# Zero products and overwritten products on TensorE in the opening of a linformer-attention and mixer kernel: more of the first kind at the start, three moved by one step, fewer of the second kind

## The chip, the cores and the metric

The kernel runs on one core of a Trainium2 chip. The metric is the device time of one execution in microseconds (us); the lower, the better. Runs of the kernel before took 430.44 to 431.93 us, with a median of 431.54 us over five runs.

## The reference

Two blocks follow each other for a batch of 8 sequences of 1024 rows, with 8 heads of 64 columns (512 columns in all):

```
k_proj = E @ k            # E, F: 64 x 1024; per batch and head 64 x 64
v_proj = F @ v
attn   = softmax(q @ k_proj^T / 8)         # 1024 x 64 per head
x      = attn @ v_proj                     # heads side by side: 1024 x 512
h      = relu(x^T @ w_tok1) @ w_tok2       # mixing over the 1024 rows
u      = x + h^T
out    = u + relu(u @ w_ch1) @ w_ch2       # mixing over the 512 columns
```

Inputs and output are float32; the kernel's products are in bfloat16 with float32 sums.

## The kernel before, in words

All inputs come in by DMA queues: E on SP's, F on ScalarE's, and everything else on GpSimd's queue, which casts float32 to bfloat16 on the way. Batch 0 comes in four head pairs; for each pair k, then q, then v, 256 KB each as stored. After the last pair come w_tok1 and w_tok2, the first half of w_ch1, and then the loads of batch 1, the rest of w_ch1 and w_ch2. The q load of batch 1 reuses the buffer of batch 0's q, so it waits for the last turn of that q.

The order of the work is written out by hand in `ORDER` (lines 17 ff.); each name stands for a small step, and every engine takes its own instructions from it in this order. Batches overlap: the up and down products of batch b run between the attention and the row mixing of the batches after it. Batch 0 has no earlier batch to run beside, so its opening runs by head pair (number after the dot):

- `EF` (`eft`, L232): eight TensorE transposes of E and F, cast to bfloat16 by VectorE (L239) and ScalarE (L240), into PSUM, and one VectorE copy to `EFT` (L233).
- `KP` and `VP` (L246, L251): eight products each of `EFT` with k or v, 64 output rows wide, for one head pair. `Ka` copies the k projection out to `kprojs`, `KT` transposes it (L271), `Ba` and `Bd` put it into the block-diagonal `kbd`. `Va` and `Vd` put the v projection into `vbd`.
- `QT` (L401): eight transposes of q; `QC` copies them out (`qT`).
- `S0`, `S1` (L455): scores of a head; `E0`, `E1`: exponential on ScalarE; `O0`, `O1` (L300): product with `vbd`, and the division on VectorE (L306, L307), into `x_sb`.
- `M1` (L470), `N0`, `N1` (L483), `UT` (L497): the row mixing of one pair's columns with w_tok1 and w_tok2, and transposes of its result; `F0` to `F3` and the steps `m0.n` (L538): the products with w_ch1.

Two kinds of products on TensorE have results that nobody reads. `busy` (L227) multiplies a part of the still zero `kbd` with itself, 512 columns, into a PSUM bank of its own: eight times at the very start, as soon as `kbd` is cleared, and three times in the step `W1`. And `FILL` (L422) gives a number of 512-column products of `EFT` with the identity (L437) for a `KP` or `VP` step: they write into the very bank that the step then starts anew, so they are overwritten. They come in front of the step's own products, whose first one waits for the load.

Of the kernel before, what the change touches and what calls it, by code (L numbers as in the profile page):

```python
# [14 lines left out]


ORDER = """
EF KP.0 Ka.0 W1 KT.0 Ba.0 Bd.0 QT.0 KP.1 QC.0 VP.0 Ka.1 S1.0 QT.1 KT.1 QC.1 VP.1 lv2 Bd.1 Ba.1
Vd.0 KP.2 S0.0 Va.0 E1.0 Vd.1 O1.0 Ka.2 QT.2 Va.1 KT.2 S0.1 E0.0 S1.1 E1.1 QC.2 Ba.2 Bd.2 O0.0
VP.2 E0.1 S0.2 KP.3 Va.2 E0.2 Vd.2 O1.1 S1.2 Ka.3 O0.1 E1.2 KT.3 Bd.3 QT.3 QC.3 VP.3 O1.2 Ba.3  # L20
S0.3 Vd.3 O0.2 E0.3 M1.0 RR.0 M1.1 RR.1 Va.3 S1.3 O0.3 M1.2 N1.0 U1.0 N0.0 U0.0 E1.3 O1.3 RR.2
# [71 lines left out]
def kernel(  # L93
# [16 lines left out]
    KP = E.shape[0]  # L110
# [111 lines left out]
    def busy(psf, n):  # L222

        zero = kbd.rearrange("p h k -> p (h k)")
        w_ps = psf("w_ps")
        for _ in range(n):
            nc.tensor.matmul(w_ps, zero[:, 0:P], zero[:, 0:512], start=True, stop=True)  # L227
# [4 lines left out]
            nc.tensor.transpose(e_ps[:, si * P : (si + 1) * P], EF_sb[:, si::SC], ident)  # L232
        nc.vector.tensor_copy(out=EFT.rearrange("p s k -> p (s k)"), in_=e_ps)  # L233

    busy(c_ps, 8)

    first = work.tile([P, 1], BF16, tag="first", name="first", bufs=1)
    nc.scalar.activation(out=first, in_=kbd[:, 0, 0:1], func=ACT.Copy)
# [173 lines left out]
    def first_ps(name, dt=F32):  # L412

        return pinned_ps(name, dt) if pinned["on"] else any_ps(name, dt)
# [4 lines left out]
        st["qT", 0] = work.tile([P, H, 4, P], BF16, tag="qT", name="qT", bufs=1)  # L419


    FILL = {("KP", 1): 4, ("KP", 2): 2, ("KP", 3): 2, ("VP", 3): 3}  # L422

    def first_op(op, hp, eng="A"):

# [8 lines left out]
        elif op in ("KP", "VP"):  # L434
            st[key(op)] = ps_ = first_ps("kv_ps")
            for _ in range(FILL.get((op, hp), 0)):
                nc.tensor.matmul(  # L437
# [476 lines left out]
```

## Time and profile before

| what | value |
|---|---|
| median of five runs | 431.54 us (430.44 to 431.93) |
| the profiled execution | 431.93 us |
| its span, first to last instruction | 430.1 us |
| TensorE busy | 416.3 us (97% of the span) |
| VectorE, ScalarE, GpSimd busy | 302.3, 203.5, 205.5 us |
| mean granted TensorE clock | 0.992 |
| chain that ended last | TensorE 92%, VectorE 4%, DMA 1% |
| DMA | 60.79 MB, mean 141 GB/s |

The chain is found by going back from the last instruction, at each step to what released it. The granted clock is the share of full speed that TensorE's throttle let through. Matmuls are pipelined, so that the duration of a single one (0.38 us for 512 columns at full speed) is longer than the time from one start to the next; a row of several in the chain shows the latter. In a list of stretches, the columns after the limits are the length, the busy time of an engine with the number of its instructions, the clock, the DMA share (over 1 where transfers overlap), and GB/s.

### The profile page before, as it was taken

The numbers are of one execution on the slowest core, as the hardware profiler recorded it, in microseconds if no ns is written. First come the engines' busy times: TensorE is split into PE (matmuls) and PEld (weight loads), VectorE is DVE, ScalarE is ACT, GpSimd is POOL, SyncE is SP. The second block draws the span as 40 slices with busy tenths as digits, with TensorE's granted clock in tenths as the row PEclk, the third lists the DMA queues.
The fourth block names the chain that finished last, engine by engine and source line by source line (L and its number), as shares of the span: only waits on it lengthen the run. The fifth ranks groups of instructions, "written<-read, shape, count | busy, mean of one in ns | idle before, by whom it ended". The sixth has DMA issues, their size and how long they took to land.

```text
span 430.1 us, 7705 instructions
## 1 busy us (share of the span) xinstructions
PE 416.3 (97%) x3034; PEld 271.9 (63%) x3066; DVE 302.3 (70%) x510; ACT 203.5 (47%) x362; POOL 205.5 (48%) x148
## 2 busy tenths in 40 slices
PE   6989999999999999999999999999999999999996
PEld 2667457765478644785457844786448854785485
DVE  2466468868936778868768677777779766947862
ACT  2436684157553555334753366334652356314621
POOL 8250014144652648553565635535356626654652
PEclk8899999999999999999999999999999999999999
DMA  9999999969979999952999289464914320242014
GB/s 168 208 206 205 207 165 175 211 131 212 202 109 203 158 240 174 168 98 50 250 170 215 91 152 155 73 171 96 163 37 90 107 99 2 53 146 98 2 49 148
DMA packets 89332, 60.79 MB, mean 141 GB/s; under 512 B 55760, under 2 KB 84944, under 8 KB 89296
## 3 DMA queue, kind: packets, MB, share of 16 engines
q0 software_dynamic: 29200, 29.36, 43.7%
q1 hardware_dynamic: 60016, 30.68, 30.2%
q8 instruction: 24, 0.39, 0.4%
q10 hardware_dynamic: 80, 0.26, 0.3%
q14 instruction: 12, 0.10, 0.1%
HBM read 59.24 MB, written 16.78 MB: 177 GB/s over the span
## 4 chain that ended last, share of the span: by engine, by line
PE 92%; DVE 4%; DMA 1%; issue 1%; ACT 1%; POOL 0%; DVEq 0%; ACTq 0%
PE be L661 19%; PE be L606 17%; PE ga L661 9%; PE ga L606 9%; PE h_ps L347 5%; PE u_ps L363 5%; PE g_ps L538 5%; PE al L661 4%; PE al L606 4%; PE kv_ps L246 4%; PE ou_ps L300 4%; PE sco L287 2%; DMA EF_in<-in_F_dram 1%; DVE S L530 1%; PE qt_ps L401 1%; PE u_ps L483 1%
## 5 line engine op out<-in xcount | busy, mean ns | idle before, releaser
L570 ACT ACTIVATE K<-be 128x512 f32<-128x512 f32 x116 | 65.7, 598 | 66.1 <-PE be L661 38.6
L661 PEld LDWEIGHTS <-g 128*128 128x128 bf16 x768 | 74.5, 98 | 16.2 <-issue 1.0
L661 PEld LDWEIGHTS <-S 128*128 128x128 bf16 x576 | 55.9, 98 | 11.7 <-issue 0.4
L292 ACT ACTIVATE attnT<-sco 128x512 bf16<-128x512 f32 x56 | 33.5, 598 | 50.8 <-PE sco L287 39.2
L606 PEld LDWEIGHTS <-wc 128*128 128x128 bf16 x336 | 32.1, 98 | 36.2 <-DVE g L612 0.4
L697 POOL TENSOR_TENSOR K<-K,u_sb 128x512 f32<-128x512 f32 x16 | 19.0, 1186 | 67.6 <-ACT K L570 67.6
L661 PE MATMUL be<-wc,g 128*128 128x256 bf16 x384 | 48.5, 273 | 0.7 <-DVE g L528 0.6
L570 ACT ACTIVATE K<-ga 128x512 f32<-128x512 f32 x58 | 32.8, 600 | 33.4 <-PE ga L661 29.9
L307 DVE TENSOR_TENSOR x_sb<-ou_ps,rdn 128x512 bf16<-128x512 f32 x64 | 44.2, 691 | 2.2
L606 PE MATMUL be<-uT,wc 128*128 128x512 bf16 x168 | 44.7, 379 | 0.2
L366 DVE TENSOR_TENSOR u_sb<-u_ps,x_sb 128x512 bf16<-128x512 f32 x56 | 37.1, 683 | 9.4 <-PE u_ps L363 8.1
L606 PEld LDWEIGHTS <-uS 128*128 128x128 bf16 x252 | 23.9, 98 | 25.7
L612 DVE CUSTOM_DVE_ANT_0 g<-be,K 128x512 bf16<-128x512 f32 x42 | 27.3, 687 | 16.7 <-PE be L606 16.6
L524 POOL TENSOR_TENSOR S<-g 128x1024 bf16<-128x1024 bf16 x7 | 14.9, 2124 | 46.6 <-DVE g L612 46.6
L645 ACT ACTIVATE g<-be 128x512 bf16<-128x512 f32 x42 | 23.8, 596 | 26.1 <-PE be L606 26.1
L528 POOL TENSOR_TENSOR g<-g 128x1024 bf16<-128x1024 bf16 x13 | 28.9, 2227 | 14.2 <-DVE S L524 14.0
L612 DVE CUSTOM_DVE_ANT_0 g<-al,K 128x512 bf16<-128x512 f32 x42 | 27.6, 687 | 10.9 <-PE al L606 10.6
L707 POOL TENSOR_TENSOR K<-K,u_sb 128x512 f32<-128x512 f32 x16 | 20.5, 1283 | 30.0 <-ACT K L570 30.0
L363 PE MATMUL u_ps<-R_sb,wt 128*128 128x512 bf16 x104 | 29.9, 379 | 0.6 <-DVE u_sb L366 0.3
L306 DVE RECIPROCAL rdn<-ou_ps 128x8 f32<-128x8 f32 x64 | 13.1, 204 | 24.6 <-PE ou_ps L300 24.3
L530 POOL TENSOR_TENSOR S<-g,S 128x1024 bf16<-128x1024 bf16 x13 | 28.4, 2187 | 0.9 <-ACT K L570 0.7
L347 PE MATMUL h_ps<-x_sb,wt 128*128 128x512 bf16 x102 | 28.1, 379 | 0.3
(102 smaller groups left out, 777.4 us busy)
## 6 DMA issues: line engine op xcount, KB each, us to landing
out_dram<-o SPq DMA_DIRECT2D x30, 512.0 KB, 3.1
q_sb<-in_q_dram POOLq DMA_DIRECT2D x7, 1024.0 KB, 11.4
k_sb<-in_k_dram POOLq DMA_DIRECT2D x7, 1024.0 KB, 11.7
v_sb<-in_v_dram POOLq DMA_DIRECT2D x7, 1024.0 KB, 12.3
wc<-in_moe_w_ch_dram POOLq DMA_DIRECT2D x4, 384.0 KB, 13.7
wc<-in_moe_w_ch_dram POOLq DMA_DIRECT2D x2, 768.0 KB, 26.4
k_sb<-in_k_dram POOLq DMA_DIRECT2D x4, 256.0 KB, 7.0
q_sb<-in_q_dram POOLq DMA_DIRECT2D x4, 256.0 KB, 7.5
```

What stands on the lines that cost most here:

```text
L292: nc.scalar.activation(out=at, in_=sco, func=ACT.Exp, scale=scale)
L307: nc.vector.tensor_tensor(out=st["x", b][:, :, h * D : (h + 1) * D].rearrange("p (b k) d -> p b k d", b=2), in0=ov[:, :, :, 0:D], in1=rdn[ ...
L347: nc.tensor.matmul(st["h", b], wt1[:, s, t * P : (t + 1) * P], st["x", b][:, s, :], start=(s == 0), stop=(s == SC - 1),)
L363: nc.tensor.matmul(u_ps, wt2[:, t, s::SC], st["R", b][:, t, :], start=(t == 0), stop=(t == TC - 1))
L366: nc.vector.tensor_add(out=st["u", b][:, s, :], in0=u_ps, in1=st["x", b][:, s, :])
L528: eng.tensor_sub(out=a21, in0=a11, in1=a21)
L530: eng.tensor_sub(out=s4, in0=a12, in1=s2)
L570: nc.scalar.activation(out=t, in_=x, func=ACT.Copy)
L606: nc.tensor.matmul(acc, l[:, dc, i * P : (i + 1) * P], r[:, :, dc, :], start=start and dc == 0, stop=stop and dc == 1, skip_group_check=True,)
L612: nc.vector._custom_dve(TENSOR_ADD_SAT, out=o, in0=x, in1=y, s0=3.0e38, s1=0.0)
L645: nc.scalar.activation(out=g_part(b, i + e, 1, 1, 0)[:, 0], in_=be[e], func=ACT.Relu)
L661: nc.tensor.matmul(acc[:, e * HF : (e + 1) * HF], l[:, lc + c, l0 + (2 * j + e) * P : l0 + (2 * j + e + 1) * P], r[:, rc + c, r0 : r0 + HF ...
```

## The change

It alters three numbers and one position:

- the zero products at the very start become 13 instead of 8;
- the step `W1`, three zero products, stands between `EF` and `KP.0` instead of behind `Ka.0`. On TensorE its products then come after the transposes of E and F and ahead of the first k projection;
- the overwritten products become two instead of four ahead of `KP.1`, none instead of two ahead of `KP.2`, one instead of two ahead of `KP.3`; the three ahead of `VP.3` stay.

In all TensorE has as many instructions as before: five zero products more and five overwritten products fewer. The lists of the other engines and of the DMAs keep their order.

```diff
@@ ORDER @@
-EF KP.0 Ka.0 W1 KT.0 Ba.0 Bd.0 QT.0 KP.1 QC.0 VP.0 Ka.1 S1.0 QT.1 KT.1 QC.1 VP.1 lv2 Bd.1 Ba.1
+EF W1 KP.0 Ka.0 KT.0 Ba.0 Bd.0 QT.0 KP.1 QC.0 VP.0 Ka.1 S1.0 QT.1 KT.1 QC.1 VP.1 lv2 Bd.1 Ba.1
...
-    busy(c_ps, 8)
+    busy(c_ps, 13)
...
-    FILL = {("KP", 1): 4, ("KP", 2): 2, ("KP", 3): 2, ("VP", 3): 3}
+    FILL = {("KP", 1): 2, ("VP", 3): 3, ("KP", 3): 1}
```

## The prediction

> **What bounds the kernel now.** I read three views of the profile before: the chain of waits over the first 60 us, the clock by stretches, and the DMA issues one by one. Over the whole span the page gives TensorE 92% of the chain, and every slice after the first few is 9 of 10 busy, so what moves TensorE's work in the first 25 us forward moves the end, unless a load stops it. The chain, as start, duration and piece:
>
> ```profile
> 6.68 0.73 PE e_ps L232 x8
> 7.41 0.02 issue
> 7.43 0.70 DVE EFT L233
> 8.14 0.04 issue
> 8.18 1.06 PE kv_ps L246 x8
> 9.24 1.40 PE w_ps L227 x3
> 10.64 0.22 PE kt_ps L271 x2
> 10.86 0.97 PE qt_ps L401 x8
> 11.82 1.71 PE kv_ps L437 x4
> 13.53 0.67 PE kv_ps L246 x5
> ...
> 20.39 0.43 PE kv_ps L437 x2
> ```
>
> See two things. The three zero products (L227) and the four overwritten products (L437) are on the chain, 1.40 and 1.71 us. And four 512-column products take 1.71 us at 11.82, two take 0.43 us at 20.39: 0.43 us each, then 0.215. So the array runs at half speed until some time after 13.5. The stretches, as from:to, length, TensorE busy, granted clock, DMA share, GB/s:
>
> ```profile
> 0.95:4.36 3.41, 2.90 (x7) 1.00 0.61 157
> 4.36:7.77 3.41, 1.13 (x10) 1.00 1.21 197
> 7.77:11.19 3.42, 3.01 (x17) 0.50 1.22 201
> 11.19:14.60 3.41, 3.41 (x25) 0.50 1.24 206
> 14.60:18.01 3.41, 3.26 (x41) 1.00 1.24 205
> ...
> 21.43:24.84 3.41, 2.29 (x27) 1.00 1.09 207
> ```
>
> The clock is halved from 7.77 to 14.60, which are the limits I found by narrowing the stretches. The 1.00 of the first row is only the absence of a record: the zero products there begin 0.43 us apart, half speed. From 4.36 to 7.77 TensorE was busy for 1.13 us and the clock fell at its end; from 21.43 to 24.84 it was busy for 2.29 us and the clock stayed.
>
> The loads (issue time plus landing time) set the floor. The last v pair is the one that matters:
>
> ```profile
> 10.46 0.71 POOL L165 DMA_DIRECT2D v_sb<-in_v_dram  x1 [0.60 <-DMA k_sb<-in_k_dram]
> ...
> v_sb<-in_v_dram POOLq DMA_DIRECT2D x1, 256.0 KB, 11.4
> ```
>
> It lands at 10.46 + 11.4 = 21.9, and VP.3 begins at 24.51. In the same way: k of pair 1 lands at 10.2 (KP.1 begins 13.46), q of pair 1 at 11.5 (QT.1 15.01), v at 12.8 (VP.1 15.71), k of pair 2 at 14.0 (KP.2 16.81), q 15.3 (QT.2 17.83), v 16.5 (VP.2 19.43), k of pair 3 at 17.9 (KP.3 20.75), q 19.1 (QT.3 23.31). Every load is 2.5 to 4.2 us early: today TensorE is behind its loads.
>
> **What the Trainium skill says.** "TensorE: Matmul & The Clock Gate", Part 1: the array's clock is halved by default; a free-running window of some 3.4 us with enough activity gives the full clock, an idle one takes it back. The trace agrees: its limits 4.36, 7.77, 14.60 are 3.41 and 2 x 3.41 apart, and 4.36 - 3.41 = 0.95 is where the first filled window began. The same page, Part 4: a transpose on TensorE does not count as busy in the same way. The trace neither proves nor excludes it: the window that failed had 0.41 us of zero products beside 0.72 of transposes. I therefore count windows with and without them. The page gives no level of activity; the trace brackets it.
>
> **The change, part by part.**
>
> 1. *Five more zero products ahead of the turned E and F.* Before, eight begin at 1.46 and end at 4.77; TensorE then idles 1.91 us until F is loaded and cast (6.68). With the clock up at 4.36 some seven run at 0.43 and six at 0.216: 1.46 + 7 x 0.427 + 6 x 0.216 = 5.75. The idle time hides them: cost 0. If the window begins late and all run at half speed, 1.46 + 13 x 0.427 = 7.01, 0.33 past 6.68: cost between 0 and 0.35 us. I take 0. They can't gain by themselves; their use is in the window 4.36 to 7.77, which holds 1.0 us more.
>
> 2. *The three zero products (W1) go ahead of KP.0.* They now follow the transposes at 7.41 and need no EFT. TensorE waits there for the 0.70 us copy of EFT until 8.18, a hole of 0.77. At full speed 3 x 0.216 = 0.65 fits: cost 0. At half speed 1.28 overruns by 0.5. What goes: 1.40 us behind KP.0. There KT.0 would have waited for Ka.0 anyway (the cast of kprojs, 9.28 to 9.70) and could begin at 9.73 instead of 10.64, so 0.9 us is the gain at today's clock.
>
> 3. *The clock.* Busy time from 4.36 to 7.77 becomes 1.13 + 1.0 (zero products) + 0.35 (W1 before 7.77) = 2.5 us, over the 2.29 that kept it later; without transposes 1.7 against about 1.5 there. I take it that the clock stays. Then KP.0 (8.18) takes the 0.63 us that KP.2 shows, Ka.0 ends at 9.3, KT.0 at 9.45, QT.0 takes 0.45 instead of 0.97 and ends at 9.9.
>
> 4. *Fewer overwritten products.* KP.1: two instead of four, at full speed 0.43 instead of 1.71. KP.1 is ready at 10.35, its k landed at 10.2: 3.2 us earlier than 13.53. From here the loads lead: QT.1 can't begin before 11.5, VP.1 12.8, KP.2 14.0, and so on to VP.3 at 21.9. The two products ahead of KP.2 (0.32 and a 0.15 us gap) and one of two ahead of KP.3 (0.22) are gone; in this case they fall into waits for loads: gain 0. VP.3's three stay, ahead of its wait.
>
> *The sum.* From VP.3 on, TensorE has the old work in the old order: 24.51 - 21.95 = 2.6 us earlier (0.05 for the wake-up, as between F's landing and its cast). **What is late next:** w_tok1 lands at 23.9; the first product of M1.0 moves from 26.74 to 24.15, just behind it. w_tok2 lands at 26.5 (N1.0's turn, 29.86 to 27.3), the first half of w_ch1 at 30.3 (35.8 to 33.2), q of batch 1 at 35.4 (39.1 to 36.5), v of batch 1 at 49.4 (kv1 52.5 to 49.9), the last of w_ch2 at 55.6, used near 60. All clear by 0.2 us or more. The moves touch no instruction of ScalarE, GpSimd, VectorE's order or SP, and no DMA. The next batch's loads wait for TensorE and come earlier with it.
>
> The profiled execution took 431.93 us, of which 1.8 lies outside its span of 430.1. 431.93 - 2.6 = **429.3 us**. The median of the five runs is 431.54; that execution is the slowest of the five (430.44 to 431.93), as would fit windows that begin elsewhere in each run. Against the median it is 2.2 us, 0.5%. The floor by landings is the same for any phase of the window; with 0.4 us for the scatter of landings the case's own range is 428.7 to 429.9. A measurement of this kernel can tell about 0.2%, 0.86 us, from no change.
>
> **Rivals.**
>
> *B: the clock falls inside the stretch where loads lead.* From 11.19 to 14.60 there would be S1.0, QT.1, KT.1, VP.1 and half of KP.2: about 2.1 us busy, and only 1.1 without transposes. That lies between the 1.13 (0.41) that lost the clock and the 2.29 (1.5) that kept it; the removed products ahead of KP.2 stood just there. The work from 14.6 to VP.3 is 5.9 us at full speed in the 7.3 us up to 21.9. One window at half speed does 1.7 us of it: VP.3 at 22.25, 429.7 us. Two: VP.3 at 24.0, 431.4 us, no change.
>
> *C: the clock falls at 7.77 as before and returns at 14.60.* W1 ends at about 8.4, KP.1 begins at 11.9 instead of 13.5. By 14.60 the lead, 1.5 us at half speed, is worth 0.75, and the fills of KP.2 and KP.3 add 0.55: -1.3, 430.6 us. For it: the bracket is only a bracket. Against: 2.5 us busy.
>
> *D, slower: the clock falls at 7.77 and the thinned stretch can't raise it again.* The window 7.77 to 11.19 with 3.01 us busy, W1's three products in it, did not raise it; the next one, with 1.71 us of dense overwritten products, did. With two of those four gone and the rest 64-column products and transposes, it may stay low. Each further us at half speed costs 0.5 us: back at 18.01, -1.3 + 1.7 = +0.4; back at 21.43, +2.1: 434.0 us. It decides from a return later than about 18.2. For it: what is removed is just what raised the clock. Against: it needs the loss at 7.77 first.
>
> That the change does nothing it says is no rival: the instruction lists show the products moved.
>
> **How the numbers follow.** The full chain holds: 0.66. B 0.13, half of it at 429.7, half at 431.4. C 0.07, on the edge of 0.2%. D 0.14. Faster: 0.64 + 0.07 + 0.04 = 0.75; same: 0.02 + 0.06 + 0.03 = 0.11; slower 0.14. The range runs from 428.7 up to 431.6, over B and C, and leaves out D and the tails of the first case.
>
> **What would show it.** Right: the halved clock before about 5 us only, or never recorded; the zero products of L227 after 7.41 0.216 apart; KP.0 at 8.2 lasting 0.63; TensorE waiting for loads of k, q and v between 11 and 22; VP.3 at 21.9 to 22.0, M1.0 at 24.2. Wrong: a clock of 0.50 beyond 7.77 (C, D) or again after 14 (B); VP.3 after 22.5; or a later wait for w_tok1, batch 1's v or w_ch2 that takes the lead back.

## The result and the profile after

| | kernel before | changed kernel |
|---|---|---|
| median | 431.13 us (45 runs, 429.24 to 432.04) | 429.49 us (24 runs, 429.05 to 431.04) |
| profiled execution / its span | 431.93 / 430.1 us | 429.48 / 427.7 us |
| first step of VP.3, of M1.0 | 24.51, 26.74 us | 22.05, 24.28 us |

The ratio is 0.9968, with a 95% interval of 0.9959 to 0.9977: faster by 0.2 to 0.4%. Between the two profiled executions the difference is 2.45 us.

TensorE's instructions in order of time, changed kernel (start, duration from the first start to the last end, engine, line, operation, output and inputs; in brackets the idle time before, and what ended it):

```profile
1.46 4.33 PE L227 MATMUL w_ps<-kbd 128*128 128x512 bf16 x13 [1.46 <-DVE kbd L217]
6.43 0.71 PE L232 MATMUL e_ps<-ident,EF_sb 128*128 128x128 bf16 x8 [0.64 <-ACT EF_sb L240]
6.98 0.81 PE L227 MATMUL w_ps<-kbd 128*128 128x512 bf16 x3
7.93 0.63 PE L246 MATMUL kv_ps<-k_sb,EFT 128*64 128x128 bf16 x8
9.07 0.23 PE L271 MATMUL kt_ps<-ident,kprojs 64*128 64x64 bf16 x2 [0.51 <-DVE kprojs L257]
9.23 0.62 PE L401 MATMUL qt_ps<-ident,q_sb 128*128 128x128 bf16 x8
9.69 0.59 PE L437 MATMUL kv_ps<-EFT,ident 128*128 128x512 bf16 x2
10.58 0.44 PE L246 MATMUL kv_ps<-k_sb,EFT 128*64 128x128 bf16 x5 [0.30 <-DMA k_sb<-in_k_dram]
...
13.15 0.63 PE L251 MATMUL kv_ps<-v_sb,EFT 128*64 128x128 bf16 x8 [0.50 <-DMA v_sb<-in_v_dram]
14.43 0.63 PE L246 MATMUL kv_ps<-k_sb,EFT 128*64 128x128 bf16 x8 [0.64 <-DMA k_sb<-in_k_dram]
...
22.05 0.63 PE L251 MATMUL kv_ps<-v_sb,EFT 128*64 128x128 bf16 x8
...
24.28 1.95 PE L470 MATMUL h_ps<-x_sb,wt 128*128 128x128 bf16 x32
```

The 13 zero products end at 5.8, ahead of the transposes of E and F. W1 (6.98) ends at 7.8, before EFT is copied out (7.9). KP.0 takes 0.63 us instead of 1.06, so the array is at full speed. From 10.58 on, TensorE waits for loads: k, v, and k again. The chain of waits of the same execution (start, duration, piece) shows which load was the last to hold it:

```profile
7.26 8.40 DMA q_sb<-in_q_dram
15.66 0.05 issue
15.71 0.62 PE qt_ps L401 x8
...
21.47 0.65 PE kv_ps L437 x3
22.12 0.56 PE kv_ps L251 x8
```

It is q of pair 2, landing at 15.66. Behind it everything down to VP.3 is TensorE's own work or VectorE's, and VP.3's three overwritten products (0.65 us) are on the chain.

In every trace of this document in which M1.0 keeps its place, thirteen in all, the execution takes M1.0's start plus 405.2 us (405.16 to 405.21). What these kernels differ in is decided ahead of M1.0.

A reading of the clock needs care here. An execution that starts at half speed shows a recorded clock of 1.00 until the clock has first risen, so half speed is read from products (0.43 us apart at 512 columns instead of 0.215; KP 1.06 us instead of 0.63).

### The profile page after: what moved, and what is told of

It is laid out like the page before. It is cut to its first block, busy times and chain, and to the rows that moved or that the text cites. A ratio compares the mean times of both kernels' runs of the same rounds, so it can differ in the third digit from the quotient of the medians.

```text
span 427.7 us, 7706 instructions
## 1 busy us (share of the span) xinstructions
PE 413.8 (97%) x3035; PEld 270.7 (63%) x3066; DVE 302.6 (71%) x510; ACT 203.5 (48%) x362; POOL 205.7 (48%) x148
## 4 chain that ended last, share of the span: by engine, by line
PE 90%; DVE 4%; DMA 2%; POOL 2%; issue 1%; ACT 0%; DVEq 0%; ACTq 0%; POOLq 0%
PE be L661 19%; PE be L606 17%; PE ga L661 9%; PE ga L606 9%; PE h_ps L347 5%; PE u_ps L363 5%; PE g_ps L538 5%; PE al L661 4%; PE al L606 4%; PE ou_ps L300 4%; PE kv_ps L246 3%; PE sco L287 2%; DMA q_sb<-in_q_dram 2%; DVE S L530 1%; PE u_ps L483 1%
## 5 line engine op out<-in xcount | busy, mean ns | idle before, releaser
L528 POOL TENSOR_TENSOR g<-g 128x1024 bf16<-128x1024 bf16 x13 | 28.9, 2226 | 14.6 <-DVE S L524 14.3
L612 DVE CUSTOM_DVE_ANT_0 g<-al,K 128x512 bf16<-128x512 f32 x42 | 27.7, 687 | 10.5 <-PE al L606 10.2
```

Of the source, the lines that this page charges most:

```text
L528: eng.tensor_sub(out=a21, in0=a11, in1=a21)
L612: nc.vector._custom_dve(TENSOR_ADD_SAT, out=o, in0=x, in1=y, s0=3.0e38, s1=0.0)
```

## The experiments

The twelve kernels were timed in three sittings of four, each together with the kernel before. A difference is to the median of before in the same sitting (431.33, 431.31, 431.11 us). The times of before fall into two groups, and its median lies in the slower one, so that these differences read high. The ratio takes in all runs and is close to that of the means.

| kernel | median us (runs) | difference | ratio, 95% interval |
|---|---|---|---|
| 13 zero products only | 429.51 (8) | -1.82 | 0.9965, 0.9953 to 0.9978 |
| W1 moved only | 430.05 (22) | -1.28 | 0.9987, 0.9975 to 0.9999 |
| fewer overwritten only | 429.68 (11) | -1.65 | 0.9970, 0.9959 to 0.9981 |
| changed, 8 zero products | 429.97 (12) | -1.36 | 0.9973, 0.9961 to 0.9985 |
| changed, old overwritten | 429.77 (13) | -1.54 | 0.9975, 0.9965 to 0.9986 |
| changed, none overwritten | 429.25 (6) | -2.06 | 0.9959, 0.9944 to 0.9974 |
| changed, 4 more at VP.2 | 430.38 (22) | -0.93 | 0.9984, 0.9976 to 0.9992 |
| changed, 4 more at KP.2 | 429.66 (10) | -1.65 | 0.9966, 0.9955 to 0.9977 |
| no zero and no overwritten products | 429.10 (6) | -2.01 | 0.9956, 0.9941 to 0.9971 |
| 13 zero products, nothing else | 429.50 (7) | -1.61 | 0.9973, 0.9951 to 0.9996 |
| w_tok2 loaded ahead of pair 3 | 434.93 (6) | +3.82 | 1.0096, 1.0077 to 1.0115 |
| w_tok1 and M1 early | 429.90 (15) | -1.21 | 0.9972, 0.9961 to 0.9983 |

### Each part alone

**13 zero products only.**

```diff
-    busy(c_ps, 8)
+    busy(c_ps, 13)
```

> The kernel before with 13 zero products at the start instead of 8; W1 and the overwritten products as before. Theory A (the clock, then the loads): the five more fill the window ahead of E and F in most executions, the clock stays up from about 4 to 7 us on, KP.0 takes 0.63 us, W1's three fit into the wait for Ka.0 and KP.1's four take 0.86 us; from 11 us on the loads lead and KP.2's and KP.3's products stand in waits: about 2 us below before's median of 431.1, within 0.3 us of the changed kernel, and most executions close together. Theory B (the gain is what left the chain: W1 behind KP.0 and five overwritten products, whatever the clock does): the five lie in TensorE's wait for F and nothing leaves the chain, so 0 us.

-1.82 us: theory A. In its trace KP.0 takes 0.63 us, W1 begins at 8.66 and ends ahead of KT.0 at 9.41, and VP.3 begins at 22.34. Raising the clock is enough, with all the old products still there.

**W1 moved only.**

```diff
-EF KP.0 Ka.0 W1 KT.0 ...
+EF W1 KP.0 Ka.0 KT.0 ...
```

> The kernel before with only W1's three zero products moved ahead of KP.0; 8 zero products at the start, overwritten products as before. Theory A: the window still fails in most executions (0.35 us of W1 more in it at most), the clock is down from 7.8 us; W1 overruns the wait for EFT by 0.2 to 0.5 us and leaves 0.9 us behind KP.0: 0.2 to 0.7 us faster, with the spread of the kernel before. Theory B: the whole 0.9 us.

The medians differ by 1.28, more than either theory said, but the 22 runs lie in two groups, sixteen from 429.25 to 430.53 and six from 431.57 to 432.47; the ratio's interval reaches almost to 1. In its trace (430.53 us) the zero products, E and F, W1 and KP.0 (1.06 us) all run at half speed, and at 10.2 the clock comes up, since KT.0 takes 0.23 us and QT.0 0.62. W1 in the wait for EFT left no hole between 6.35 and 9.69, where the kernel before has one of 0.78 us. That the filled hole is what raised the clock fits this trace and that of the changed kernel with eight zero products (full speed from 10.0); it was not tested apart. The clock is not what sets this trace's time: M1.0 begins 1.05 us later than in the changed kernel, of which 0.83 is the landing of q of pair 2 (16.49 instead of 15.66) and 0.22 the one product more ahead of KP.3.

**Fewer overwritten products only.**

```diff
-    FILL = {("KP", 1): 4, ("KP", 2): 2, ("KP", 3): 2, ("VP", 3): 3}
+    FILL = {("KP", 1): 2, ("VP", 3): 3, ("KP", 3): 1}
```

> The kernel before with only the overwritten products thinned (2, 0, 1 and 3 instead of 4, 2, 2 and 3). Theory A: those of KP.1 are what raised the clock at 14.6; with fewer of them it returns later in many executions: between 1.4 us faster (returns as before) and 2 us slower, the median near 0 or slower, with a wide spread. Theory B: 2 x 0.43 at half speed and 0.55 at full speed leave the chain: 1.4 us faster.

-1.65 us, all 11 runs within 429.39 and 430.29: near theory B's 1.4, and none of A's spread. Its profiled execution is the slowest of these, and it ran at half speed down to about 14 us:

```profile
8.54 1.06 PE L246 MATMUL kv_ps<-k_sb,EFT 128*64 128x128 bf16 x8 [0.79 <-DVE EFT L233]
9.54 1.46 PE L227 MATMUL w_ps<-kbd 128*128 128x512 bf16 x3
...
11.97 1.06 PE L437 MATMUL kv_ps<-EFT,ident 128*128 128x512 bf16 x2
...
14.44 0.61 PE L401 MATMUL qt_ps<-ident,q_sb 128*128 128x128 bf16 x8
...
22.88 0.63 PE L251 MATMUL kv_ps<-v_sb,EFT 128*64 128x128 bf16 x8
```

The clock rose with two of the four products gone that I had taken for its cause, and VP.3 is only 0.83 us behind the changed kernel. No load is on the chain of this slowest of the runs behind F; the median, 0.61 us shorter, stands for an M1.0 at about 24.5 (an estimate, 429.68 less 405.2).

By the medians the three parts alone give 1.82 + 1.28 + 1.65 = 4.75 us, and together 1.64; by the means 1.52 + 0.68 + 1.34 = 3.54, and together 1.37. So they are not three savings that add up but three ways to much the same floor. In the traces of the first two it is the landing of q of pair 2.

### Undoing one part

**Eight zero products in the changed kernel** (`busy(c_ps, 13)` back to 8).

> The changed kernel with 8 zero products at the start instead of 13, all else as changed. Theory A: the clock falls at the end of the window about F's arrival in most executions and the thinned stretch raises it late: 1 to 3.5 us above the changed kernel's 429.5, so about 430.5 to 433, with a wide spread. Theory B: as the changed kernel, 429.5.

0.5 us above the changed kernel's median (0.28 by the differences to before), runs from 428.98 to 431.13: nearer to B. The half speed that A expected is in its trace (KP.0 1.06 us at 8.44, full speed from KT.0 at 10.01), but VP.3 begins at 22.27, only 0.22 us later than in the changed kernel.

**The old overwritten products in the changed kernel** (the `FILL` line of before).

> The changed kernel (13 zero products, W1 ahead of KP.0) with the overwritten products of the kernel before (4, 2, 2, 3 instead of 2, 0, 1, 3). Theory A (with the clock up from the start the loads lead, and only what stands behind q of pair 2, landing at 15.7, costs its time): KP.1's two more end at 10.55, as its k lands; KP.2's two lie in the wait for k of pair 2; KP.3's one more costs 0.22: 429.7. Theory B (every overwritten product on TensorE costs its time): five times 0.216, 430.6.

429.77: theory A. Five products cost 0.28 us, not 1.1.

**None overwritten** (`FILL = {}` in the changed kernel).

> The changed kernel with no overwritten products at all (six fewer). Theory A: KP.1's two and KP.3's one stand in waits for k; VP.3's three (0.65 us) stand ahead of a v that landed at 21.5, while VP.3 begins at 22.05; w_tok1 at 24.0 stops M1.0 (24.28 in the changed kernel): 0.2 to 0.3 faster, 429.2, if the clock stays. Theory B: 1.3 us faster, 428.2. Theory C (these products hold the clock through the stretch where the loads lead): the clock falls between 11 and 25 us in a part of the executions, 0.5 to 2 us slower.

429.25: theory A. No run lies above 429.78. In its chain w_tok1 holds M1.0:

```profile
12.19 12.27 DMA wt<-in_moe_w_tok_dram
24.46 0.05 issue
24.50 1.96 PE h_ps L470 x32
```

### The floor

**Four more overwritten products, ahead of VP.2 and ahead of KP.2.**

```diff
-    FILL = {("KP", 1): 2, ("VP", 3): 3, ("KP", 3): 1}
+    FILL = {("KP", 1): 2, ("VP", 2): 4, ("VP", 3): 3, ("KP", 3): 1}    # one kernel
+    FILL = {("KP", 1): 2, ("KP", 2): 4, ("VP", 3): 3, ("KP", 3): 1}    # the other
```

> The changed kernel with four overwritten products added ahead of VP.2, behind the last load that the chain shows (q of pair 2, 15.7 us). Theory A (from there on TensorE is the bound again): the whole 0.86 us, 430.3. Theory of the prediction (v of pair 3 is the gate, VP.3 waits for it): up to 0.2 us, 429.6.

> The changed kernel with four overwritten products added ahead of KP.2, in the 0.64 us that TensorE waits for k of pair 2 there, ahead of the gate at 15.7. Theory A: 0.86 - 0.64 = 0.2 late at KP.2, 0.1 to 0.2 of which the wait for q of pair 2 takes up: 0 to 0.1 us, 429.5. Theory B: 0.86 us, 430.3. Theory C: they hold the clock in the few executions in which it falls, so that those above 430 us become fewer.

The same four products cost 0.89 us behind q of pair 2 and 0.17 us ahead of it; the two kernels, timed in one sitting, lie 0.72 us apart. So from 15.7 on the bound is TensorE's own row of work, with VectorE's divisions in it, and the prediction's gate, v of pair 3, is not it. Of the 10 runs at KP.2, two lie above 430, against four of the changed kernel's 24, so that the hope of theory C, fewer such runs, is not met.

In its trace the 13 zero products stay at half speed and end only at 7.19, so that the transposes of E and F begin at 6.98. KP.1 still waits 0.20 us for its load, so that none of this delay reaches the end.

**w_tok2's load ahead of pair 3's loads.**

```diff
         for name, src in ((("k", k), ("q", q), ("v", v))):
             load(0, name, src, hs)
...
+        if hp == 2:
+            nc.gpsimd.dma_start(out=wt2, in_=moe_w_tok2.rearrange("(tc p) s -> p tc s", p=P))
         if hp == 3:
...
-    nc.gpsimd.dma_start(out=wt2, in_=moe_w_tok2.rearrange("(tc p) s -> p tc s", p=P))
```

> The changed kernel with one alteration on GpSimd's queue: the load of w_tok2 (512 KB, about 2.5 us of transfers) is issued ahead of pair 3's k instead of last. TensorE's work is the same. Theory A (the loads of pair 3 and w_tok1 are the floor): k, q and v of pair 3 and w_tok1 land 2.5 us later, M1.0 at 26.6 instead of 24.3: 2.0 to 2.4 us slower, 431.7. Theory B (TensorE's own products are the bound): 0 to 0.3 us.

5.4 us above the changed kernel, where A expected 2.0 to 2.4. TensorE by stretch (from:to, length, busy, granted clock, DMA share, GB/s), and two lines of its instructions (line numbers are one more than in the kernel before):

```profile
15.00:18.00 3.00, 2.92 (x36) 1.00 1.20 211
18.00:21.00 3.00, 0.66 (x5) 1.00 1.19 205
21.00:22.00 1.00, 0.16 (x2) 0.86 1.23 202
22.00:24.00 2.00, 1.83 (x13) 0.50 1.22 225
24.00:26.00 2.00, 1.48 (x14) 0.50 1.07 196
26.00:28.00 2.00, 2.00 (x11) 0.50 1.30 202
28.00:30.00 2.00, 1.19 (x12) 0.86 1.24 173
```

```profile
18.28 0.38 PE L438 MATMUL kv_ps<-EFT,ident 128*128 128x512 bf16 x1
21.84 1.01 PE L247 MATMUL kv_ps<-k_sb,EFT 128*64 128x128 bf16 x8 [3.18 <-DMA k_sb<-in_k_dram]
```

KP.3 begins at 21.84 instead of 18.29: 3.55 us from the load. In the idle 3.18 us ahead of it the clock fell and stayed at half for about 6.8 us. M1.0 is 5.89 us later (30.17 instead of 24.28); I put the other 2.3 us down to the clock, but no run took the two apart. A late load is the floor, and a long wait for it costs the clock as well. All six runs show a mean clock of 0.988 to 0.992, as in no other kernel here.

### What the dead products are worth

**No zero and no overwritten products at all** (both `busy` calls and `FILL` emptied).

> The changed kernel without any zero product (neither the 13 nor W1) and without any overwritten product: only the work that counts. Theory A (the clock is worth something up to the load floor): the clock is down until about 14 to 18 us; KP.0 at 8.5 at half speed, KP.1 at about 11.2, and at 14 to 18 TensorE is 1 to 2.5 us behind the loads: 430.3 to 432. Theory B (only the count of products on the chain matters): as without overwritten products, 429.2 or below.

429.10, all six runs from 428.94 to 429.29: theory A fails, B holds. This is the fastest median and, in six runs, the tightest spread of all. Its TensorE, in order of time (line numbers from 235 on are one less than in the kernel before):

```profile
6.57 1.07 PE L232 MATMUL e_ps<-ident,EF_sb 128*128 128x128 bf16 x8 [6.57 <-ACT EF_sb L239]
8.43 1.06 PE L245 MATMUL kv_ps<-k_sb,EFT 128*64 128x128 bf16 x8 [0.78 <-DVE EFT L233]
10.00 0.29 PE L270 MATMUL kt_ps<-ident,kprojs 64*128 64x64 bf16 x2 [0.51 <-DVE kprojs L256]
10.22 1.04 PE L400 MATMUL qt_ps<-ident,q_sb 128*128 128x128 bf16 x8
...
13.02 1.06 PE L400 MATMUL qt_ps<-ident,q_sb 128*128 128x128 bf16 x8
...
15.82 0.61 PE L400 MATMUL qt_ps<-ident,q_sb 128*128 128x128 bf16 x8
...
21.56 0.63 PE L250 MATMUL kv_ps<-v_sb,EFT 128*64 128x128 bf16 x8
...
23.81 1.96 PE L469 MATMUL h_ps<-x_sb,wt 128*128 128x128 bf16 x32
```

It is at half speed down to about 15, and yet QT.2 begins at 15.82 against 15.71 in the changed kernel, and VP.3 at 21.56 against 22.05. Its chain holds no load behind F: at half speed the work that counts comes to QT.2 0.5 us after q of pair 2 has landed (15.28), and makes that up where no product stands ahead of KP.3 and VP.3. It comes to M1.0 (23.81) when w_tok1 has just landed (23.74), so that a faster clock would have gained next to nothing in this trace.

The loads of these traces land at different times though they are issued in the same order: q of pair 2 between 15.3 and 16.5, w_tok1, where its place in the queue is the old one, between 23.7 and 24.5. In this trace both land earlier than in any other. Differences of some tenths of a us between single traces can be that alone.

**The 13 zero products, and nothing else** (`W1` and `FILL` out of the changed kernel).

> The changed kernel without W1's three zero products and without any overwritten product; the 13 zero products stay. Theory A (W1 ahead of KP.0 costs nothing, and the 13 alone hold the clock): as with W1 and no overwritten products, 429.25 within 0.2. Theory C (W1 is needed to carry the clock over the wait for EFT): the clock falls in a part of the executions, median or spread up by 0.5 to 1.5 us.

Median 429.50, but one of seven runs took 432.61, with a mean clock of 0.990, and two others show 0.994 and 0.995; in the kernel that differs by W1 alone (none overwritten) all six runs lie at 0.998 or above. That points to theory C: raised early and then left idle, the clock may fall. Seven runs don't settle it.

**w_tok1 and M1 early** (from the changed kernel without overwritten products).

```diff
-        if hp == 3:
+        if hp == 2:
             nc.gpsimd.dma_start(out=wt1, in_=moe_w_tok1.rearrange("(p si) t -> p si t", p=P))
...
-VP.2 E0.1 S0.2 KP.3 Va.2 E0.2 Vd.2 O1.1 S1.2 Ka.3 O0.1 E1.2 KT.3 Bd.3 QT.3 QC.3 VP.3 O1.2 Ba.3
-S0.3 Vd.3 O0.2 E0.3 M1.0 RR.0 M1.1 RR.1 Va.3 S1.3 ...
+VP.2 E0.1 S0.2 Va.2 E0.2 Vd.2 O1.1 S1.2 O0.1 E1.2 M1.0 RR.0 KP.3 Ka.3 O1.2 KT.3 Bd.3 QT.3 QC.3 O0.2 M1.1 RR.1 VP.3 Ba.3
+S0.3 Vd.3 E0.3 Va.3 S1.3 ...
```

> A try at a better version: the changed kernel without overwritten products, with w_tok1's load ahead of pair 3's loads, and M1.0 and M1.1 moved in ORDER into the waits for pair 3 (M1.0 ahead of KP.3, M1.1 ahead of VP.3). Theory A (the loads are the floor and TensorE's waits in front of them can take 2.7 us of M1): v of pair 3 lands at 24.0 and is the last gate; behind it stand some 1.5 us fewer: 427.8. Rival (VectorE's divisions and copies, in whose order M1 waits, or the clock, become the bound): 429 or more.

429.90: a miss. M1.0 and M1.1 do run early (20.35 and 23.72). The last load on the chain is not v of pair 3 but k, which lands at 21.47 instead of 18.28 because w_tok1 is loaded ahead of it. VP.3 comes behind M1.1, at 24.70, and behind M1.1 the chain is a row of short steps:

```profile
24.81 0.38 ACT R_sb L475
25.19 0.17 ACT kbd L255
25.36 0.05 issue
25.40 0.40 PE sco L455
...
25.89 0.61 ACT attnT L462
26.50 0.05 issue
26.54 0.40 PE ou_ps L300 x4
```

ScalarE's copy to kbd comes behind M1.1's relu in its order, then scores, exponential and O follow with nothing beside them: M1.2 begins at 26.78, against 26.51 in the changed kernel.

## Why the prediction was right, and where not

- **The time.** 429.3 forecast, 429.49 measured. Working from the profiled execution, 2.6 us forecast, 2.45 found. The way there was right (the loads lead), the load that holds TensorE was another (part 4), so the closeness is in part luck.
- **Size against the median.** 0.5% forecast, 0.23 to 0.41% measured. The failed term is the base: the median of five runs, 431.54, was high. Over 45 runs it is 431.13, and the 40 and 38 runs of the first two sittings lie in two groups, 429.9 to 430.8 and 431.0 to 432.1. The profiled execution is at the upper end. I noted that it was the slowest of five and made nothing of it. It is a rare kind too: its recorded clock, 0.992, came in 3 of the 99 runs of the three sittings. The course of the clock from which I counted (up at 4.36, down at 7.77, back at 14.60) may be that of few executions; no other one of this kernel has a trace.
- **Part 1, zero products at no cost:** right in this trace. They end at 5.8, ahead of the transposes of E and F at 6.43.
- **Part 2, W1 in the wait for EFT:** right; KT.0 at 9.07 (9.45 forecast).
- **Part 3, the clock stays up:** right for the changed kernel's trace; with its zero products back at eight, the trace is at half speed until 10.
- **Part 4, the loads lead:** right, and shown by the costs of 0.17 and 0.89 us. The gate was misplaced: q of pair 2 at 15.7, not v of pair 3. The step failed at "VP.3's three stay, ahead of its wait". They end at 22.1, behind v's landing at 21.5 (10.83 + 10.7), and so stand on the chain. The lines of before could have shown that the two gates were nearly level. From QT.2 (17.83) to VP.3 (24.51) went 6.68 us at full speed, with a division on VectorE in the chain:

```profile
21.75 0.22 DVE rdn L306
...
22.00 0.70 DVE x_sb L307
...
23.93 0.65 PE kv_ps L437 x3
24.58 0.56 PE kv_ps L251 x8
```

Less one product (0.22), 6.46 us behind a q that landed at 15.3 is 21.8, against 21.95 for v: only 0.14 us of wait. The 5.9 us of work that rival B sets against 7.3 us are about TensorE's busy time; the waits come on top, some 1.1 us from 14.6 to VP.3 in the changed kernel's trace (6.3 busy of 7.45), 0.90 of them for VectorE's division. In the changed kernel's trace q landed 0.3 us later and v 0.3 us earlier, and the order of the two gates turned round. That 22.05 is so near to 21.95 was in part luck.
- **What is late next:** right. w_tok1 is what stops M1.0 in the traces of the two kernels with the 13 zero products and no overwritten ones (landing at 24.46 and 24.25).
- **Rivals B and C** did not occur in the changed kernel's trace. Of its 24 runs one, 431.04 us at a clock of 0.994, may be such a case.
- **Rival D** rested on the reading that the overwritten products are what raises the clock. The kernels with fewer or none speak against it: thinned, the slowest run was 430.29; with none and no zero products, 429.29. Its 434.0 was met by no run with these loads; the longest, 432.47 and 432.61, belong to kernels that keep all the overwritten products or all 13 zero products, at mean clocks of 0.994 and 0.990.
- **What I had not seen:** how little the clock is worth here. Up to VP.3 the chain of before holds 4.5 us of products whose results nobody reads (1.40 of L227; 1.71, 0.32, 0.43 and 0.65 of L437), and the loads were 2.5 to 4.2 us ahead. I took the loads as the floor for the fast clock only. The kernel without any such product comes to that floor with half speed down to about 15. Raising the clock makes the dead products cheap; leaving them out makes the clock nearly unimportant in this opening.

The kernel with none of them has the lowest median here, 0.9956 of before. Its interval (0.9941 to 0.9971) overlaps that of the changed kernel (0.9959 to 0.9977), and the two were not timed in one sitting, so that its lead of 0.4 us over the changed kernel is likely, not certain. The changed kernel without overwritten products (0.9959, 2.06 us below its before, against 2.01) can't be told from it.

## What to carry to other kernels

Products that only keep TensorE's clock up are paid for wherever they stand on the chain; before adding or moving them, compare each step's start with the landing of its load, and try the kernel with none. When each part of a change alone gives nearly the whole gain, they lead to a common floor: look for it among the landings, and see whether the next landing is only some tenths of a us behind. A single profiled execution may belong to one of two groups of times, so take the base from many runs.

## What the runs showed of the hardware

- Executions that began at half speed show a mean recorded clock of 1.000: the kernel without zero products, at half speed to about 15 us, and the kernel with only W1 moved, at half speed to 10 us.
- In the kernel before, 56 of the 60 runs of 431.0 us and above have a recorded clock of 1.000, and 33 of the 39 faster ones 0.995 or 0.996. Between these two kinds the higher recorded mean went with the longer time.
- The clock rose with real work alone, 64-column products, transposes and scores, at about 15 us in the kernel without zero products. An idle wait of 3.18 us lost it for about 6.8 us in the kernel with w_tok2 loaded early.
- Eight transposes took 1.04 us (QT.0) while the array was at half speed and 0.61 us (QT.2) at full speed, in the kernel without zero products.
- The same load, issued in the same order, landed at different times from trace to trace: q of pair 2 between 15.3 and 16.5 us.
